# Dynamic convolution, FFT mixing and MLP on one core: the opening's DMA order, the second step's evictions, and the first three groups' transposition changed

## The chip, the cores and the metric

One NeuronCore of a Trainium2 chip runs the whole kernel. The metric is the device time of one execution in microseconds. Its engines are TensorE (PE), VectorE (DVE), ScalarE (ACT), GpSimd (POOL) and SyncE (SP), the last of which issues DMAs. Each works through its own list of instructions in order.

## The reference

x is 8 batches of 4224 positions by 192 channels; weight_gen gives 7 taps for each of 8 heads of 24 channels at every position.

```python
w = exp(weight_gen - max over taps); w = w / (sum over taps + 1e-9)
x = sum over 7 taps of w[b, s, head] * x_pad[b, s + tap, head's channels]
u = x + real(fft over channels(fft over positions(x)))
un = (u - mean(u)) / sqrt(var(u) + 1e-6)          # over the 192 channels
out = u + relu(un @ w_ch1) @ w_ch2                # 192 -> 768 -> 192
```

## The kernel before

The 4224 positions are laid out as 128 partitions by 33 rows. A batch is cut into groups of four rows (512 positions); nine groups make a batch, the last with one row, so there are 72 groups, counted through.

- `conv(b)`: the softmax of the taps (`softmax_taps`, L488 to L498), the products of taps and x (L656 on VectorE, L624 on ScalarE, L654 on GpSimd) and their sums (L666, mostly on GpSimd; in the first batch also in matmuls against the identity into pa, L662). Then row pairs are added and subtracted (sm, L680 and L682), and pg (L687) is the transform over the 128 partitions; the result is turned into gt (L694, L697) and stored to `g_d` in DRAM.
- `transform(b)`, "the second step": loads `g_d` as g2 (L722), transforms it in pp (L732) and evicts pp into the table pq, with a mirrored part and for e = 1 a sign (L736, L741, L743, L746, all on ScalarE).
- `mix(b, g)`: eo (L761) is the transform over the channels, one matmul a row and a part, added to u (ot on ScalarE at L766, then L767, L768, L770, L771 on VectorE).
- `norm(b, g)`: mean and variance (L795, L796), the root (L804), its reciprocal (L805), a shift (L808) and the normalized rows un (L813). For the MLP un is split into fp16 hi and lo parts: hl (hi at L821 on ScalarE, lo at L822 and L824), which one DMA transposes into ht (L830). For the first three groups (`QUICK`) un lies in PSUM and VectorE makes lo; later un is in SBUF and GpSimd makes it.
- `mlp(n)`: per group six chunks of 128 hidden channels. A chunk is five ph matmuls of 128x512 (L855), relu into hh (L861 for the first seven groups), then po (L878) and, at the end, u is completed (L883) and stored (L887). The first seven groups take fp32 hh and w2.

The weights are prepared in the opening: `prep_w1` rebuilds w1 from its words (L413 to L424, seven VectorE operations for a piece of 128x384), splits it into w1h and w1l (L429 ScalarE, L430 VectorE) and copies a part of it between partitions by DMA (L456). `prep_w2` does the same words for the three pieces of w2. Raw words share buffers with hl, un and ht.

The order on each engine is fixed beforehand: the generators are advanced in a written order, which sets data and buffer dependences; `held` and `behind` tie instructions to others; then `plan` places every instruction by a list scheduler with a table of costs (`cost`), and the lists it makes are what the engines run. PSUM has banks named fft (2), ph (3), po (2) and wp (1). Warm matmuls, whose results nobody reads, stand in three places (L709): 20 before the second step, 12 beside group 0's hl, 12 before group 1's MLP.

Of the kernel before, what the change touches and what calls it, by code (L numbers as in the profile page):

```python
# [46 lines left out]
F32_GROUPS = 7  # L47
ACT_TAPS = {(0, 1): (0,), (0, 3): (0,), (0, 5): (0,1), (0, 7): (0,)}
TURNS = {1: 'ddpdddd', 2: 'dpddpdd', 3: 'dpddpdp'}
WARM = (20, 0, 12, 12)  # L50
# [64 lines left out]
def cost(ins, lane, reads, writes):  # L115

    count = lambda ap: int(np.prod([n for _, n in ap.ap[1:]]))
    out = writes[0]
    n = max(map(count, reads + writes))
    if lane == "pe":  # L120
        n = count(out)
        t = 2 * max(112 if 64 < n <= DH else 56, 0.846 * n) if reads[0].dtype == F32 else max(55.5, 0.4205 * n + 0.4)
# [12 lines left out]
    return (t + 100, t + 90) if len(writes) > 1 else (t - 95, t)  # L135


def plan(nc, tc, homes, holds):
# [38 lines left out]
    spare = {row: [0.0] * homes[names[0]][2] for row, names in rows.items()}  # L177
# [110 lines left out]
def tile_dynconv_fnet_mlp(  # L288
# [158 lines left out]
    def prep_w1(raws):  # L447
        s1 = weight_scale([raw[:, :, 1] for raw in raws], 64, "w1")
        scales.append(s1)
        hi, lo = temp("w1h_1", F16), temp("w1l_1", F16)  # L450
        w = words_to_f32(raws[0], None, "w1_1", ("ph", 3))
        split_f32(w, hi, lo, s1)
        for src, dst in ((hi, w1h1), (lo, w1l1)):
            for i in range(2):
                for j in range(2):
                    nc.sync.dma_start(dst[64 * j:64 * j + 64, i * PW:(i + 1) * PW], src[64 * i:64 * i + 64])  # L456
# [61 lines left out]

    def conv(b):
# [34 lines left out]
        if b == 0:  # L554
            need_x(NC)
            need_x(0)
            tap_step(0, 7)
            need_x(1)
            need_x(3)
            load_consts()  # L560
        groups = [(NC, 0), (1, 2), (3, 4), (5, 6), (7,)] if b == 0 else [(c,) for c in range(NC + 1)]
# [142 lines left out]

    def keep_warm(bank, nm, lhsT, rhs, count):

        spare = pst(*bank, [P, 512], F32, f"warm_{nm}")
        for _ in range(count):
            nc.tensor.matmul(spare[:, 0:rhs.shape[-1]], lhsT=lhsT, rhs=rhs, start=True, stop=True)  # L709

    def transform(b):
# [5 lines left out]
        for m0 in range(0, NM, TRI):  # L717
# [4 lines left out]
            last_g2[b] = nc.sync.dma_start(g2[:, 0:full], bass.AP(first.tensor, first.offset, [[D, WL], [W * D, full], [1, D]]))  # L722
# [4 lines left out]
            for e, (tab, d0) in enumerate(((te_sb, 0), (to_sb, D - DH))):  # L727
# [8 lines left out]
                nc.scalar.copy(rows[:, k0:k0 + nk, :], pp[0:DH, 0:nk, 0:NT])  # L736
# [3 lines left out]
                if e == 0:  # L740
                    nc.scalar.copy(dst, src)  # L741
                else:
                    nc.scalar.mul(dst, src, -1.0)  # L743
# [4 lines left out]
    state, us, hls, products = {}, {}, {}, []  # L748
    last_tile, last_pg, last_product, last_fold, last_gt, last_g2, last_pp = {}, {}, {}, {}, {}, {}, {}
    pending = {}  # L750
    total = B * NG

    def mix(b, g):
# [4 lines left out]
        for e in range(2):  # L758
            for j in range(J):
                r = 2 * g + 1 + j if g < NC else 0  # L760
                nc.tensor.matmul(eo[:, e, j, :], lhsT=pq[0:DH, e, r, r:r + P], rhs=cs_sb[:, e, :],  # L761
                                 start=True, stop=True)
                yield 0.1 * (J * e + j + 1)
# [15 lines left out]
    def norm(b, g):  # L779
# [7 lines left out]
        if quick:  # L787
            halves = [pst("ph", 3, [P, 2, D], F32, f"un_{b}_{g}_{i}") for i in range(2)]
        else:
            un = sb.tile([P, 4, D], F32, tag="un", name=f"un_{b}_{g}", bufs=1)  # L790
            halves = [un[:, 0:2], un[:, 2:4]]
# [14 lines left out]
        if sign < 0:  # L806
            for t in range(T):
                nc.vector.tensor_scalar(out=rs[:, 1, t:t + 1], in0=st[:, t, 0:1], scalar1=rs[:, 0, t:t + 1], scalar2=sign,  # L808
                                        op0=ALU.mult, op1=ALU.mult)
        else:  # L810
            nc.gpsimd.tensor_tensor(out=rs[:, 1, 0:T], in0=st[:, 0:T, 0], in1=rs[:, 0, 0:T], op=ALU.mult)  # L811
        for t in range(T):
            nc.scalar.activation(halves[t // 2][:, t % 2, :], uv[:, t, :], AF.Identity,  # L813
                                 bias=rs[:, 1, t:t + 1], scale=rs[:, 0, t:t + 1])
        yield 0.5
        warm = NG * b + g == 0
        hl = sb.tile([P, 4, 2 * D], F16, tag="hl", name=f"hl_{b}_{g}", bufs=2)
        lo_eng = nc.vector if NG * b + g < QUICK else nc.gpsimd
        spans = [(un, 0, T)] if NG * b + g >= QUICK else [(h, 2 * i, 2 * i + 2) for i, h in enumerate(halves)]
        for src, t0, t1 in spans:  # L820
            nc.scalar.copy(hl[:, t0:t1, 0:D], src[:, 0:t1 - t0, :])  # L821
            lo_eng.tensor_tensor(out=hl[:, t0:t1, 2 * P:3 * P], in0=src[:, 0:t1 - t0, 0:P],  # L822
                                 in1=hl[:, t0:t1, 0:P], op=ALU.subtract)
            last_lo[NG * b + g] = lo_eng.tensor_tensor(out=hl[:, t0:t1, D:2 * P], in0=src[:, 0:t1 - t0, P:D],  # L824
                                                       in1=hl[:, t0:t1, P:D], op=ALU.subtract)
        if warm:
            keep_warm(("ph", 3), f"hl{g}", hl[:, 0, 0:P], hl[:, T - 1, 0:2 * D], WARM[2])
        hls[NG * b + g] = hl
# [102 lines left out]
    with held(last_pg[0].ins):  # L931
        WARM[0] and keep_warm(("po", 2), "pp", ident32, last_tile[0][:, 3, 0:P], WARM[0])
    add(0.0, 1.0, transform(0))
    run()
    lp = last_product[0].ins
# [5 lines left out]
    queue(lp, (prep_w1, loaded[0]))  # L941
    for i in range(2):
        queue(last_split[-1].ins, (prep_w2, i))
    for g in range(QUICK):
        add(0.0, 1.0, behind(last_split[-1].ins, mix(0, g)))
        run()
        add(0.0, 1.0, norm(0, g))
        run()
    for g, call in ((0, tap8), (1, (prep_w2, 2)), (1, tap9)):
# [14 lines left out]
    def late_warm(g):  # L964
        yield 0.0
        with held(last_ph[g - 1].ins):
            keep_warm(("ph", 3), f"hl{g}", hls[g][:, 0, 0:P], hls[g][:, 3, 0:2 * D], WARM[3])

# [11 lines left out]
    add(0.93, 0.95, late_warm(1))  # L980
# [52 lines left out]
```

## Time and profile before

| | us |
|---|---|
| median of 3 runs | 1126.27 |
| runs | 1126.01, 1126.27, 1127.51 |
| the profiled execution | 1124.56 |
| its span in the profile | 1122.8 |
| mean granted TensorE clock in it | 0.983 of full |

The page gives each engine's busy time, then the span in 40 slices, DMA queues, the chain that ended last and the costliest groups of instructions. A timeline row reads: start, length, engine, line, operation, what it writes, what it reads, shape, count, and in brackets the idle time before it with what ended that. A row of fp32 matmuls counts two passes for each matmul in its last number. Waits read: who waited for whom, the sum, how often, the longest. The profiled execution's own time is 1.76 us more than its span, and 1.71 us under the median.

### The profile page before, as it was taken

The numbers are of one execution on the slowest core, as the hardware profiler recorded it, in microseconds if no ns is written. First come the engines' busy times: TensorE is split into PE (matmuls) and PEld (weight loads), VectorE is DVE, ScalarE is ACT, GpSimd is POOL, SyncE is SP. The second block draws the span as 40 slices with busy tenths as digits, with TensorE's granted clock in tenths as the row PEclk, the third lists the DMA queues.
The fourth block names the chain that finished last, engine by engine and source line by source line (L and its number), as shares of the span: only waits on it lengthen the run. The fifth ranks groups of instructions, "written<-read, shape, count | busy, mean of one in ns | idle before, by whom it ended". The sixth has DMA issues, their size and how long they took to land.

```text
span 1122.8 us, 23426 instructions
## 1 busy us (share of the span) xinstructions
PE 1077.9 (96%) x8476; PEld 825.0 (73%) x8476; DVE 969.8 (86%) x1773; ACT 817.8 (73%) x2415; POOL 876.7 (78%) x759
## 2 busy tenths in 40 slices
PE   5986899999999999999999999999999999999998
PEld 2565487678777877787778877777778777787777
DVE  7987999779989999899999999899989999455543
ACT  4475766658986787778786888778787878689842
POOL 4979699699996999699997999599987999311200
PEclk9897799999999999999999999999999999999999
DMA  8334244533384246614474246623454222513321
GB/s 318 120 106 146 43 110 126 148 102 106 86 221 120 65 106 164 176 59 103 117 204 117 78 121 178 162 58 101 119 158 114 71 61 71 145 43 75 72 47 47
DMA packets 156500, 128.71 MB, mean 115 GB/s; under 512 B 108571, under 2 KB 133088, under 8 KB 156384
## 3 DMA queue, kind: packets, MB, share of 16 engines
q1 hardware_dynamic: 156384, 127.21, 41.6%
q8 instruction: 67, 1.10, 0.4%
q14 instruction: 49, 0.40, 0.1%
HBM read 61.46 MB, written 39.37 MB: 90 GB/s over the span
## 4 chain that ended last, share of the span: by engine, by line
PE 77%; DVE 10%; POOL 5%; issue 3%; ACT 3%; DMA 1%; SPq 0%; DVEq 0%; ACTq 0%; POOLq 0%
PE ph L855 33%; PE po L878 30%; PE eo L761 5%; PE pp L732 5%; POOL u L666 4%; PE pg L687 3%; DVE pr L656 3%; ACT pr L624 1%; PE pa L662 1%; DMA g<-g_d 1%; DVE u L666 1%; DVE u L656 1%; ACT w L491 1%; POOL sm L680 0%; DVE u L883 0%
## 5 line engine op out<-in xcount | busy, mean ns | idle before, releaser
L666 POOL TENSOR_TENSOR u<-u,pr 128x768 f32<-128x768 f32 (+1 forms) x396 | 655.5, 1673 | 53.5 <-DVE pr L656 46.2
L878 PE MATMUL po<-w2h,hh 128*128 128x192 f16 x2832 | 421.6, 246 | 0.0
L878 PEld LDWEIGHTS <-hh 128*128 128x128 f16 x4248 | 364.5, 98 | 68.2
L855 PE MATMUL ph<-ht,w1h 128*128 128x512 f16 (+1 forms) x1296 | 400.0, 363 | 3.0 <-ACT hh L861 1.5
L656 DVE TENSOR_TENSOR pr<-x_sb,wp 128x768 f32<-128x768 f32 (+1 forms) x415 | 354.0, 876 | 20.8 <-POOL u L666 16.4
L878 PE MATMUL po<-w2l,hh 128*128 128x192 f16 x1416 | 348.1, 246 | 0.0
L866 DVE SCALAR_TENSOR_TENSOR hh<-ph,hh 128x512 f16<-128x512 f32 (+1 forms) x390 | 245.1, 634 | 78.5 <-ACT hh L865 77.3
L855 PE MATMUL ph<-ht,w1l 128*128 128x512 f16 (+1 forms) x864 | 311.4, 363 | 0.0
L865 ACT ACTIVATE hh<-ph 128x512 f16<-128x512 f32 (+1 forms) x390 | 214.6, 553 | 118.7 <-PE ph L855 84.1
L855 PEld LDWEIGHTS <-w1h 128*128 128x128 f16 x1296 | 126.6, 99 | 85.8 <-DVE hl L824 2.3
L813 ACT ACTIVATE un<-u,rs 128x192 f32<-128x192 f32 x264 | 124.0, 535 | 26.6 <-POOL rs L811 21.3
L822 POOL TENSOR_TENSOR hl<-un,hl 128x512 f16<-128x512 f32 (+1 forms) x69 | 74.4, 1078 | 61.3 <-ACT hl L821 30.7
L855 PEld LDWEIGHTS <-w1l 128*128 128x128 f16 x864 | 85.7, 99 | 45.5 <-issue 3.3
L802 ACT ACTIVATE junk<-u,st 128x192 f16<-128x192 f32 x252 | 113.7, 451 | 3.8
L800 ACT ACTIVATE junk<-u 128x192 f16<-128x192 f32 x252 | 90.6, 360 | 25.3 <-DVE u L771 20.9
L761 PE MATMUL eo<-cs_sb,pq 97*128 97x97 f32 x544 | 90.8, 274 | 3.4 <-DVE u L771 3.4
L761 PEld LDWEIGHTS eo<-cs_sb,pq 97*128 97x128 f32 x544 | 83.5, 193 | 12.3 <-issue 3.6
L883 DVE SCALAR_TENSOR_TENSOR u<-po,isc,u 128x384 f32<-128x384 f32 (+1 forms) x122 | 72.7, 596 | 7.4 <-PE po L878 7.0
L680 POOL TENSOR_TENSOR sm<-u 128x382 f32<-128x382 f32 x64 | 64.3, 1005 | 7.5 <-ACT u L675 7.5
L811 POOL TENSOR_TENSOR rs<-st,rs 128x4 f32<-128x4 f32 (+1 forms) x69 | 15.4, 223 | 65.6 <-DVE rs L805 65.6
L736 ACT COPY pq<-pp 97x204 f32<-97x204 f32 (+1 forms) x96 | 46.5, 484 | 25.4 <-PE pp L732 24.2
L878 PE MATMUL po<-w2f,hh 128*128 128x192 f32 x336 | 63.8, 327 | 0.0
(108 smaller groups left out, 1295.5 us busy)
## 6 DMA issues: line engine op xcount, KB each, us to landing
out_dram<-u SPq DMA_DIRECT2D x64, 384.0 KB
x_sb<-in_x_dram SPq DMA_DIRECT2D x48, 384.0 KB
g<-g_d SPq DMA_DIRECT2D x40, 336.0 KB
x_sb<-in_x_dram SPq DMA_DIRECT2D x8, 864.0 KB
g_d<-gt SPq DMA_DIRECT2D x32, 195.0 KB
g_d<-gt SPq DMA_DIRECT2D x32, 189.0 KB
w<-in_weight_gen_dram SPq DMA_DIRECT2D x6, 924.0 KB
x_sb<-in_x_dram SPq DMA_DIRECT2D x8, 672.0 KB
```

What stands on the lines that cost most here:

```text
L656: last_product[b] = nc.vector.tensor_tensor(out=dst, in0=rows, in1=wk, op=ALU.mult)
L666: adder.tensor_tensor(out=u, in0=u, in1=pr, op=ALU.add)
L761: nc.tensor.matmul(eo[:, e, j, :], lhsT=pq[0:DH, e, r, r:r + P], rhs=cs_sb[:, e, :], start=True, stop=True)
L800: nc.scalar.activation(junk, uv[:, t, :], AF.Identity, scale=-1.0 / D, accum_out=st[:, t, 0:1])
L802: nc.scalar.activation(junk, uv[:, t, :], AF.Square, bias=st[:, t, 0:1], accum_out=st[:, t, 1:2])
L813: nc.scalar.activation(halves[t // 2][:, t % 2, :], uv[:, t, :], AF.Identity, bias=rs[:, 1, t:t + 1], scale=rs[:, 0, t:t + 1])
L822: lo_eng.tensor_tensor(out=hl[:, t0:t1, 2 * P:3 * P], in0=src[:, 0:t1 - t0, 0:P], in1=hl[:, t0:t1, 0:P], op=ALU.subtract)
L855: last_ph[n] = nc.tensor.matmul(ph[:, 0:T], lhsT=wt[:, cs_], rhs=ht[:, 0:T, blk], start=(i == 0), stop=(i == len(terms) - 1))
L865: nc.scalar.activation(a[:, 0:T], ph[:, 0:T], AF.Relu)
L866: nc.vector.scalar_tensor_tensor(out=l[:, 0:T], in0=ph[:, 0:T], scalar=0.0, in1=a[:, 0:T], op0=ALU.max, op1=ALU.subtract)
L878: nc.tensor.matmul(po[t // 2][:, t % 2, :], lhsT=hx[:, t], rhs=wx[:, c2, :], start=(c2 == 0 and i == 0), stop=(c2 == NH - 1 and i == len(t ...
L883: nc.vector.scalar_tensor_tensor(out=lt, in0=po[t // 2][:, 0:t % 2 + 1], scalar=scales[0][:, 1:2] if f32 else isc, in1=lt, op0=ALU.mult, o ...
```

## The change

The arithmetic of the result stays. What moves:

1. The planner lets the first two weight_gen loads go before the first x load on SP (`spare` starts at -1e3), and its TensorE costs change slightly.
2. Warm matmuls: 14 (identity by identity) at the very start, 40 instead of 20 before the second step, and these wait for the last pg alone, not for gt; 8 each after the mixes of groups 1 and 2; the 24 by hl go.
3. The eight w1h and w1l copies on SP stand behind the g2 load of m0 = 8.
4. In the first batch, for e = 1, the mirrored and the third copy of pp into pq go from ScalarE to VectorE (8 operations).
5. A root of one column, whose result is not used, makes ScalarE load the root's table right after the last of its pq copies.
6. The order of the first mixes and norms is written by hand: mix 1, mix 2 and their warm matmuls are issued among norm 0; w2's first two pieces use ph banks and hang on the first split of w1 instead of the last; the large softmax steps of the second batch follow groups 1 and 2 instead of 0 and 1.
7. Norm of groups 0 to 2: un lies in SBUF, two of its rows are made by ScalarE and two by VectorE; eight fp32 matmuls against the identity transpose it into two po banks; ScalarE casts these to ht's hi part and VectorE subtracts to give lo. There is no hl and no DMA transposition for these groups.

```diff
-    spare = {row: [0.0] * homes[names[0]][2] for row, names in rows.items()}
+    spare = {row: [-1e3] * homes[names[0]][2] for row, names in rows.items()}
...
-        for src, dst in ((hi, w1h1), (lo, w1l1)):
+        with held(g2_loads[0, 2 * TRI].ins):
+            for src, dst in ((hi, w1h1), (lo, w1l1)):
...
-        words_to_f32(loaded[1][i], w2_part(i)[0], f"w2_{i}", ("po", 2))
+        words_to_f32(loaded[1][i], w2_part(i)[0], f"w2_{i}", ("ph", 3) if i < 2 else ("po", 2))
...
+            if b == 0 and WARM.get(grp[0]):
+                with held(last_pg[0].ins):
+                    keep_warm(pst("po", 2, [P, P], F32, f"warm_{grp[0]}"), WARM[grp[0]])
...
+                on_dve = b == 0 and e == 1
+                last_pq[b] = nc.scalar.copy(rows[:, k0:k0 + nk, :], pp[0:DH, 0:nk, 0:NT])
...
+                elif on_dve:
+                    nc.vector.tensor_scalar_mul(out=dst, in0=src, scalar1=-1.0)
...
-                    nc.scalar.copy(rows[:, P + k0:P + k0 + n, :], pp[0:DH, 0:n, 0:NT])
+                    (nc.vector.tensor_copy if on_dve else nc.scalar.copy)(rows[:, P + k0:P + k0 + n, :], pp[0:DH, 0:n, 0:NT])
...
+        if quick:
             for t in range(T):
+                if t < ACT_ROWS:
+                    nc.vector.tensor_scalar(out=rs[:, 1, t:t + 1], ...)
+                    nc.scalar.activation(un[:, t, :], uv[:, t, :], AF.Identity, bias=rs[:, 1, t:t + 1], scale=rs[:, 0, t:t + 1])
+            for t in range(ACT_ROWS, T):
+                nc.vector.tensor_scalar(out=un[:, t, :], in0=uv[:, t, :], scalar1=st[:, t, 0:1], scalar2=rs[:, 0, t:t + 1],
+                                        op0=ALU.subtract, op1=ALU.mult)
+            yield 0.5
+            ht = sb.tile([P, 4, 3, P], F16, tag="ht", name=f"ht_{b}_{g}", bufs=3)
+            tr = [pst("po", 2, [P, 4, P], F32, f"tr_{b}_{g}_{i}") for i in range(2)]
+            R = D - P
+            for i, m in ((0, P), (1, R)):
+                for t in range(T):
+                    nc.tensor.matmul(tr[i][0:m, t, :], lhsT=un[:, t, i * P:i * P + m], rhs=ident32, start=True, stop=True)
+                nc.scalar.copy(ht[0:m, 0:T, i], tr[i][0:m, 0:T])
+                at = P - m
+                last_lo[NG * b + g] = nc.vector.tensor_tensor(out=ht[at:P, 0:T, 2 - i], in0=tr[i][0:m, 0:T],
+                                                              in1=ht[0:m, 0:T, i], op=ALU.subtract)
...
+    with held(last_pq[0].ins):
+        nc.scalar.activation(sb.tile([P, D], F16, tag="junk", name="root", bufs=2)[:, 0:1], eps_t, AF.Sqrt)
...
+    step(mixes[0])
+    step(norms[0], 1)
+    warm = pst("po", 2, [P, P], F32, "warm_eo")
+    for g in range(1, QUICK):
+        step(mixes[g], 4)
+        with held(last_mix[0].ins):
+            keep_warm(warm, WARM_EO[g - 1])
+    step(norms[0])
     for i in range(2):
-        queue(last_split[-1].ins, (prep_w2, i))
...
+        queue(last_split[0].ins, (prep_w2, i))
+    for g in range(1, QUICK):
+        step(mixes[g])
+        step(norms[g])
+        if g == 1:
+            queue(last_split[0].ins, (prep_w2, 2))
+    for g, call in zip(TAPS_AT, (tap8, tap9)):
         queue(last_lo[g].ins, call)
```

Three places show what the planner made of it. First SP, before the second step of the first batch: before, three copies of w1h stand ahead of the first g2 loads (names: `g2_0_m` is the load for m0 = m).

```order
L701 DMA g_d0_95<-gt_0_6_596 63x768
L456 DMA w1h1_89<-w1h_1_880 64x384 x3
L722 DMA g2_0_0_702<-g_d0_95 112x4x192
L722 DMA g2_0_4_720<-g_d0_95 112x4x192
L722 DMA g2_0_8_738<-g_d0_95 112x4x192
L456 DMA w1h1_89<-w1h_1_880 64x384
L456 DMA w1l1_90<-w1l_1_881 64x384 x4
L722 DMA g2_0_12_754<-g_d0_95 112x4x192
```

After, on the same engine:

```order
L712 DMA g_d0_95<-gt_0_6_611 63x768
L730 DMA g2_0_0_737<-g_d0_95 112x4x192
L730 DMA g2_0_4_755<-g_d0_95 112x4x192
L730 DMA g2_0_8_773<-g_d0_95 112x4x192
L460 DMA w1h1_89<-w1h_1_917 64x384 x4
L460 DMA w1l1_90<-w1l_1_918 64x384 x4
L730 DMA g2_0_12_789<-g_d0_95 112x4x192
```

The first three g2 loads follow the last store at once, and all eight copies stand behind them. Second TensorE, from the first mixes to the MLP, before (each of the 12 warm matmuls has its own weight load).

```order
L761 MATMUL eo_0_0_946<-cs_sb_70,pq_71 128x97 x4
L761 MATMUL eo_0_1_1003<-cs_sb_70,pq_71 128x97 x4
L761 MATMUL eo_0_2_1047<-cs_sb_70,pq_71 128x97 x4
L709 LDWEIGHTS hl_0_0_981
L709 MATMUL warm_hl0_988<-hl_0_0_981 128x384
```

After, on TensorE:

```order
L773 MATMUL eo_0_0_963<-cs_sb_70,pq_71 128x97 x4
L773 MATMUL eo_0_1_996<-cs_sb_70,pq_71 128x97 x4
L526 MATMUL warm_eo_995<-ident32_72 128x128 x8
L773 MATMUL eo_0_2_1009<-cs_sb_70,pq_71 128x97 x4
L526 MATMUL warm_eo_995<-ident32_72 128x128 x8
L829 MATMUL tr_0_0_0_1023<-ident32_72,un_0_0_977 128x128
L829 MATMUL tr_0_0_1_1024<-ident32_72,un_0_0_977 64x128
L829 MATMUL tr_0_0_0_1023<-ident32_72,un_0_0_977 128x128 x3
L829 MATMUL tr_0_0_1_1024<-ident32_72,un_0_0_977 64x128 x3
```

The first ph follows the transposes at once; group 1's transposes stand behind 13 ph matmuls of group 0, and group 2's behind the second chunk of group 1. pg_1_4 moves from 4.20 to 4.40 groups of MLP work, pp of batch 2 from 14.83 to 15.17, and pp of batch 7 stays at 60.33. Third VectorE in the second step, after; before, no row of pp stands on this engine.

```order
L752 TENSOR_SCALAR pq_71<-pp_0_0_1_747 97x11x17
L757 COPY pq_71<-pp_0_0_1_747 97x12x17
L433 SCALAR_TENSOR_TENSOR w1l0_88<-pw_w1_01_952,sc_w1_914,w1h0_87 128x384
L419 TENSOR_SCALAR pa_w2_0_1037<-raw_w3_428 128x384
L420 SCALAR_TENSOR_TENSOR pw_w2_0_1038<-pa_w2_0_1037,t_w2_0_1039 128x384
L416 TENSOR_SCALAR pa_w2_1_1047<-raw_w4_431 128x384
L752 TENSOR_SCALAR pq_71<-pp_0_4_1_765 97x12x17
L757 COPY pq_71<-pp_0_4_1_765 97x4x17
```

The eight copies stand between the words of w2's first two pieces, which came after pp before. On ScalarE, group 2's un (L819) stands between hh_0_0_0 and hh_0_0_1, and ot_0_3 ahead of hh_0_0_0.

More of the change, by code (lines that the diff above doesn't have):

```diff
@@ L517, in mirrored, with keep_warm @@
         return bass.AP(ap.tensor, ap.offset, [ap.ap[0], [step, 2], *ap.ap[1:]])
+    def keep_warm(spare, count):
+        for _ in range(count):
+            nc.tensor.matmul(spare, lhsT=ident32, rhs=ident32, start=True, stop=True)
     def conv(b):
@@ L760, in mix @@
                 r = 2 * g + 1 + j if g < NC else 0
[L761 removed]
+                last_mix[b] = nc.tensor.matmul(eo[:, e, j, :], lhsT=pq[0:DH, e, r, r:r + P], rhs=cs_sb[:, e, :],
                                  start=True, stop=True)
@@ L786, in norm @@
         quick = NG * b + g < QUICK
[L787 to L791, printed above, removed]
+        un = sb.tile([P, 4, D], F32, tag="un", name=f"un_{b}_{g}", bufs=1)
         if quick or (b > 0 and g in BN_GROUPS):
@@ L819, in norm @@
[L819 to L825, printed above, removed]
@@ L941, in tile_dynconv_fnet_mlp, with step @@
     queue(lp, (prep_w1, loaded[0]))
-    for i in range(2):
-        queue(last_split[-1].ins, (prep_w2, i))
[L944 to L949, printed above, removed]
+    mixes, norms = ([f(0, g) for g in range(QUICK)] for f in (mix, norm))
+    def step(gen, n=99):
+        for _, at in zip(range(n), gen):
+            pass
+    step(mixes[0])
[6 more added lines that the diff above has]
+    step(norms[0])
+    for i in range(2):
+        queue(last_split[0].ins, (prep_w2, i))
[5 more added lines that the diff above has]
+    for g, call in zip(TAPS_AT, (tap8, tap9)):
         queue(last_lo[g].ins, call)
```

55 lines of the change are left out of this document (25 added, 30 removed).

## The prediction

> **What bounds the kernel now.** I read the page first: how much of the span TensorE fills.
>
> ```profile
> span 1122.8 us, 23426 instructions
> PE 1077.9 (96%) x8476; PEld 825.0 (73%) x8476; DVE 969.8 (86%) x1773; ACT 817.8 (73%) x2415; POOL 876.7 (78%) x759
> ```
>
> Then the busy time by stretch, to see where the missing 45 us lie (columns: stretch, its length, each engine's busy time, granted clock, DMA share, GB/s).
>
> ```profile
> 80.00:100.00 20.00, 16.68 (x122) 15.89 (x121) 13.21 (x26) 10.00 (x26) 20.00 (x14) 0.78 0.60 165
> 100.00:120.00 20.00, 8.76 (x43) 5.71 (x42) 19.08 (x67) 11.74 (x27) 20.00 (x13) 0.65 0.27 79
> 120.00:140.00 20.00, 18.46 (x89) 11.00 (x90) 19.84 (x37) 13.22 (x35) 10.48 (x10) 0.84 0.26 40
> 400.00:1123.00 723.00, 719.83 (x6163) 556.62 (x6160) 610.42 (x1106) 552.16 (x1598) 536.14 (x475) 1.00 0.40 106
> ```
>
> From 400 us on TensorE idles 3 us in 723; between 80 and 140 us it idles 16, at a reduced clock. So after the opening the time is TensorE's work, and the kernel ends as much earlier as the MLP begins earlier, less whatever TensorE then has to wait for. Next come TensorE's waits from 75 to 360 us, and its timeline there.
>
> ```profile
> PE warm_hl L709 <- DVE st L796: 6.6, 1, 6.6
> PE pp L732 <- DMA g<-g_d: 4.7, 4, 2.7
> ```
>
> ```profile
> 79.19 6.12 PE L709 MATMUL warm_pp<-gt,ident 128*128 128x128 f32 x40 [1.23 <-DVE gt L697]
> 88.02 0.91 PE L732 MATMUL pp<-te_sb,g 102*97 102x102 f32 x8 [2.71 <-DMA g<-g_d]
> 91.71 1.57 PE L732 MATMUL pp<-to_sb,g 102*97 102x102 f32 x8
> 101.12 2.25 PE L761 MATMUL eo<-cs_sb,pq 97*128 97x97 f32 x16
> 106.05 2.00 PE L761 MATMUL eo<-cs_sb,pq 97*128 97x97 f32 x8 [2.67 <-DVE u L771]
> 119.97 0.61 PE L855 MATMUL ph<-ht,w1h 128*128 128x512 f16 x1 [1.31 <-DVE hl L824]
> 123.82 0.58 PE L855 MATMUL ph<-ht,w1h 128*128 128x512 f16 x1 [1.54 <-ACT hh L861]
> 127.30 0.36 PE L761 MATMUL eo<-cs_sb,pq 97*128 97x97 f32 x2
> 131.33 2.11 PE L709 MATMUL warm_hl<-hl 128*128 128x384 f16 x12
> 133.28 0.38 PE L855 MATMUL ph<-ht,w1h 128*128 128x512 f16 x1
> 160.07 0.38 PE L855 MATMUL ph<-ht,w1h 128*128 128x512 f16 x1
> 161.15 1.46 PE L878 MATMUL po<-w2f,hh 128*128 128x192 f32 x8
> ```
>
> The mixes of groups 0 and 1 start at 101.12, but the first MLP matmul only at 119.97: 18.9 us with a few microseconds of work in them. Group 1's first MLP matmul follows at 133.28. Between the two lie 13.3 us. At full clock five ph matmuls take 1.08 (160.07 to 161.15), so group 0's 30 take 6.5, and four eo about 0.8 (2 in 0.36 to 0.4): 7.3 us. The other 6.0 are the stall of 1.54, the 2.11 of warm_hl1, and the half clock. That the clock is halved shows in pp: 0.91 for a block, then 1.57.
>
> Last, what the first MLP matmul waits for, on the other engines' timelines.
>
> ```profile
> 82.56 1.78 SPq L456 DMA_DIRECT2D w1h<-w1h  x3
> 84.57 1.47 SPq L722 DMA_DIRECT2D g<-g_d  x3
> 95.95 0.62 DVE L430 SCALAR_TENSOR_TENSOR w1l<-pw_w,sc_w,w1h 128x384 f16<-128x384 f32 x1 [5.69 <-ACT w1h L429]
> 96.49 0.55 DVE L413 TENSOR_SCALAR pa_w<-raw_w 128x384 int32<-128x384 int32 x1
> 100.59 0.55 DVE L413 TENSOR_SCALAR pa_w<-raw_w 128x384 int32<-128x384 int32 x1
> 101.45 0.30 ACT L743 ACTIVATE pq<-pp 97x68 f32<-97x68 f32 x1
> 105.36 0.54 DVE L771 TENSOR_TENSOR u<-u,eo 128x380 f32<-128x380 f32 x1
> 107.60 0.17 DVE L796 BATCH_NORM_AGGREGATE st<-bn 128x2 f32<-128x6 f32 x1
> 108.47 1.28 ACT L804 ACT_TABLE_LOAD   x1
> 110.78 1.83 ACT L813 ACTIVATE un<-u,rs 128x192 f32<-128x192 f32 x4 [0.72 <-DVE rs L808]
> 112.54 0.84 ACT L821 CAST hl<-un 128x384 f16<-128x384 f32 x2
> 113.38 0.41 DVE L822 TENSOR_TENSOR hl<-un,hl 128x256 f16<-128x256 f32 x1
> 114.58 14.31 SPq L830 DMA_TRANSPOSE ht<-hl  x3
> ```
>
> Group 0's u is complete at 105.90, un starts at 110.78 (a table load of 1.28 sits in between), the split ends with DVE about 114.5, and the DMA transpose takes from its issue at 114.58 to 119.9: 5.3 us.
>
> **The change, part by part.** Times are those of the profiled execution.
>
> *Start.* The weight DMAs go ahead of the first x DMA. The chain of waits opens with the first row below; the last part to land decides when pa can start.
>
> ```profile
> 1.20 3.94 DMA w<-in_weight_gen_dram
> 10.19 7.25 PE pa L662 x16
> ```
>
> At best the softmax starts 2 us earlier; at worst x lands later by the same bytes and nothing comes of it. I take 1 us (0 to 2), because the products that follow also need an x piece still in flight then. The 14 warm matmuls there stand before any other TensorE work and cost nothing.
>
> *Second step.* SP no longer waits for w1h before the g2 loads, so they can issue at about 82.6 instead of 84.57, and land near 86. The 40 warm matmuls need no gt, but they stand in front of the pp: 40 at 0.235 (the 20 above took 6.12, half of that time at half clock) are 9.4, or up to 18 at half clock. From about 77 they end between 86.5 and 91; I take 87. pp then runs at full clock, but the eight moved evictions stand on VectorE between word operations. Of these the seven of w2_0 took 96.49 to 100.59, 0.585 each; 13 of them and 8 evictions at 0.3 to 0.55 are 10 to 12 us from 89, so pq is complete between 99 and 101.7, against 101.75 now. I take 101.2: nothing gained there. But the 5.69 us in which VectorE waited now hold w2's preparation, so it has none left when the mixes come, and u of group 0 is complete at about 104.9 rather than 105.9.
>
> *Norm.* The root table is loaded right after the last pq eviction, behind TensorE's eo, where ScalarE has nothing else: free by 103, and ot then starts at most 0.5 later. From u: statistics 1.9 (105.90 to 107.77 now) and 0.4 for an add of group 1 among them, root, reciprocal and two shifts 1.1 (before: 109.76 to 110.78), so un starts at 108.2 instead of 110.78. Two rows on each engine take 0.9 instead of 1.83. Eight fp32 transposes are 8 x 0.235 = 1.9, partly beside un; by eo, at 0.2 for 97 columns, 2.1; at half clock 3.8. The cast of 128x512 is near the cast row's 0.42 for 128x384, so 0.55. First ph: 108.2 + 0.5 + 1.2 + 0.6 = **110.5** instead of 119.97, 9.4 earlier.
>
> [...]
>
> *First MLP groups.* From the first ph to ph_0_1_0 TensorE now has the 7.3 us of work, transposes of group 1 (1.9), and stalls that ScalarE's order makes: hh_0_0_0 stands behind ot_0_3, which needs eo_0_3, and hh_0_0_1 behind un of group 2, which waits for VectorE. With three ph banks that is about 1.7 (0 to 5). Group 2's transposes add 1.9. So 7.3 + 1.9 + 1.7 + 1.9 = 12.8 against 13.3. **TensorE's lead is 9.4 + 0.5 = about 10 us.**
>
> *VectorE and GpSimd behind it.* VectorE gains 8 evictions (2.6), 6 rows of un (1.8, at 0.3 each) and 6 lo of 512 columns (3.8, at 0.63 each, between once and twice the 0.41 for 256 columns), and loses the old lo (6 pairs at 0.55, two of which take 113.38 to 114.5: 3.3) and six one-column shifts (about 0.8): net +4, against 5.69 of idle time now filled. The next rows show the chain that it feeds: the second batch's convolution.
>
> ```profile
> 128.08 0.94 DVE L656 TENSOR_TENSOR u<-x_sb,wp 128x768 f32<-128x768 f32 x1
> 196.96 0.22 POOL L682 TENSOR_TENSOR sm<-u 128x2 f32<-128x2 f32 x1
> 209.25 0.81 PE L687 MATMUL pg<-sm,f_sb 128*128 128x192 f32 x4
> 221.89 14.74 POOL L666 TENSOR_TENSOR u<-u,pr 128x768 f32<-128x768 f32 x8 [9.34 <-DVE pr L656]
> 850.00:950.00 100.00, 100.00 (x864) 78.47 (x863) 98.53 (x176) 80.48 (x248) 99.32 (x77) 1.00 0.27 73
> ```
>
> By the new order the first product (128.08 now) comes at about 130 to 131.5, with the mix of group 3 ahead of it that stood behind it before: 0 to 2 us later on equal terms. A sum that is ready at 197.2 is used only at 209.25, so TensorE can come up to 12 us earlier before it waits. Later the slack is thin: VectorE and GpSimd are 98 to 99% busy in the last convolution's stretch. I let TensorE give back 2 of its 10 us (0 to 8) on the way.
>
> **Sum.** 10 - 2 = 8: 1124.56 - 8 = 1116.6 for the profiled execution. That execution lay 1.7 under the median of 1126.27, so the median becomes **1118.3**.
>
> [...]
>
> **The rivals.**
>
> *All of the lead is kept* (15%). VectorE and GpSimd catch up in their idle shares (VectorE 86% over the span). 1126.3 - 10 = 1116.3, and with 2 at the start and no stalls 1113.8.
>
> *Convolution or ScalarE's order eats 4 to 7 us* (12%): pg or hh waits in the first three batches. 1126.3 - 4.5 = about 1122. For it: 98% in the quoted stretch; against: the 12 us between 197.2 and 209.25.
>
> *Half clock through the first MLP matmuls* (5%). Transposes and eo cost 1.9 more, some 3 us of ph double: 3.8 lost, 1122. It needs the 16 warm matmuls between the eo to leave a pause like the 2.67 above.
>
> *The change does little* (9%). The warm block ends at 91, the evictions wait behind word operations past 104, and the norm starts as late as now; the first ph is at 116 to 118 and stalls take the rest: 1124 to 1128.5.
>
> *Slower* (7%). The convolutions, not TensorE, set the end of each transform. VectorE starts the second convolution 3.5 late (131.6 for 128.08); busy to 98% it never catches up, and the order leaves batch 7's pp after the same share of MLP work as before, so TensorE waits there, the lead is gone and the delay shows: 1126.3 + 2.7 = 1129. It decides where the chain starts over 1 us late on equal terms and the slack of 12 us in the second batch is gone too. Against it: GpSimd's 9.34 idle before 221.89.
>
> **Chances and range.** 52% for the forecast, 1116.5 to 1120 by its own bounds. A measurement tells about 0.2% (2.25 us) from no change. Faster by more: 52 + 15 + 12 + 5 = 84%; within: 9%; slower: 7%. The range goes from the full lead, 1113.8, to 1124.5 and leaves out the slower case and most of the one where little happens, with a tail below.
>
> **What would show it.** Right: the first ph near 110.5 at full clock, no DMA transpose before it; TensorE's waits in 75 to 360 down from some 20 us to about 8; pq complete near 101; the second convolution's first product at 130 to 131.5; pp of batch 1 some 8 us earlier than 232. Wrong: idle TensorE before pg or pp of the second or third batch, ph at 0.42 each after 111, first ph after 114, or pq after 103.

## The result, and the profile after

The changed kernel takes **1138.58 us** (median of 4 runs, 1136.77 to 1139.33) against 1126.86 (4 runs, 1126.01 to 1127.51) for the kernel before: a ratio of 1.0102, 95% interval 1.0089 to 1.0115. It is 1% slower. The forecast was 1118.3. The profiled execution took 1139.18.

The head of the page, after: the span is 14.6 us longer, TensorE's and VectorE's busy times have grown by 18.7 and 16.2, and TensorE's share is the same 96%.

```profile
span 1137.4 us, 23642 instructions
PE 1096.6 (96%) x8600; PEld 837.9 (74%) x8600; DVE 986.0 (87%) x1775; ACT 813.5 (72%) x2402; POOL 876.6 (77%) x759
```

The busy time by stretch, after (same columns as above): from 100 to 120 us VectorE counts as busy for 16.90 us, but with 26 instructions where it had 67. GpSimd has no idle time there at all.

```profile
100.00:120.00 20.00, 10.37 (x81) 8.93 (x80) 16.90 (x26) 5.73 (x14) 20.00 (x13) 0.84 0.19 67
120.00:140.00 20.00, 16.33 (x78) 9.50 (x79) 18.02 (x45) 9.38 (x19) 3.42 (x5) 0.82 0.00 1
```

TensorE's waits from 75 to 360 us, after. The 6.6 us ahead of the warm matmuls on hl are gone, and the wait for g has fallen from 4.7 to 0.8; the first row is new.

```profile
PE tr L829 <- DVE un L821: 10.8, 2, 10.5
PE pg L698 <- POOL sm L693: 5.5, 5, 2.1
PE pp L740 <- DVE pq L757: 2.0, 2, 1.6
PE pp L740 <- ACT pq L757: 1.6, 2, 1.1
```

TensorE's timeline, after. pp starts at 86.98 where 87 was forecast. The transposes of group 0 begin at 110.56, stop for 10.46 us, and the first MLP matmul comes at 125.62: forecast 110.5, before 119.97. pp does not keep the full clock that was forecast: after a wait of 1.63 us for an eviction on VectorE, five blocks take 1.34 to 1.66 us, where one at full clock takes 0.86 to 0.94; the granted clock was 0.64 from 92 to 96 us and 0.50 from 96 to 100.

```profile
78.05 9.09 PE L526 MATMUL warm<-ident 128*128 128x128 f32 x80
86.98 0.86 PE L740 MATMUL pp<-te_sb,g 102*97 102x102 f32 x8
...
92.17 0.91 PE L740 MATMUL pp<-to_sb,g 102*97 102x102 f32 x8 [1.63 <-DVE pq L757]
...
94.65 1.65 PE L740 MATMUL pp<-to_sb,g 102*97 102x102 f32 x8 [0.39 <-DVE pq L757]
...
110.56 1.27 PE L829 MATMUL tr<-ident,un 128*128 128x128 f32 x6 [0.54 <-ACT un L819]
122.29 0.79 PE L829 MATMUL tr<-ident,un 128*128 128x128 f32 x2 [10.46 <-DVE un L821]
...
125.62 0.61 PE L874 MATMUL ph<-ht,w1h 128*128 128x512 f16 x1
...
129.24 2.41 PE L829 MATMUL tr<-ident,un 128*128 128x128 f32 x16
```

VectorE's timeline, after. The two rows of un that were priced at 0.3 each take 13.40 us together for group 0; group 1's two, beside an idle GpSimd (0.00 busy from 124 to 150 us), take 0.66. The statistics of the same u (first row), also from SBUF to SBUF, took 0.33 beside the same busy GpSimd. Further down is the second convolution's first product.

```profile
107.75 0.33 DVE L803 BATCH_NORM_STATS2 bn<-u 128x6 f32<-128x192 f32 x1
...
109.96 13.40 DVE L821 TENSOR_SCALAR un<-u,st,rs 128x192 f32<-128x192 f32 x2
...
127.83 0.66 DVE L821 TENSOR_SCALAR un<-u,st,rs 128x192 f32<-128x192 f32 x2
...
148.04 0.95 DVE L667 TENSOR_TENSOR u<-x_sb,wp 128x768 f32<-128x768 f32 x1
```

All six instructions of that line, after, as the view of one line gives them (shortest, median, longest in ns): one instruction of 12.278 us among others of 0.37.

```profile
L821 DVE TENSOR_SCALAR un<-u,st,rs x6: 371/375/12278, 110.0 to 135.0; 128x192 f32<-128x192 f32 x6
```

GpSimd's timeline, after, at the end of that instruction. The 12.278 us begin at 109.96 and end at 122.24, 0.12 after the end of GpSimd's L677 (122.12) and while its small L693 runs; from 100 us on GpSimd has had no idle time. The second row of un ends at 123.36, 0.11 after L691.

```profile
119.36 1.01 POOL L691 TENSOR_TENSOR sm<-u 128x382 f32<-128x382 f32 x1
120.31 1.81 POOL L677 TENSOR_TENSOR u<-u,pr 128x768 f32<-128x768 f32 x1
122.06 0.23 POOL L693 TENSOR_TENSOR sm<-u 128x2 f32<-128x2 f32 x1
122.26 0.99 POOL L691 TENSOR_TENSOR sm<-u 128x382 f32<-128x382 f32 x1
```

The 11.9 us that this instruction took beyond the shortest show neither as idle time nor in the table of VectorE's waits: VectorE counts as busy. They show in the spread between median and longest (0.375 and 12.278), and in the count of instructions in a stretch (26 for 67).

### The profile page after: what moved, and what is told of

Read it like the earlier page. It is cut to its first block, busy times and chain, and to the rows that moved or that the text cites. A ratio compares the mean times of both kernels' runs of the same rounds, so it can differ in the third digit from the quotient of the medians.

```text
span 1137.4 us, 23642 instructions
## 1 busy us (share of the span) xinstructions
PE 1096.6 (96%) x8600; PEld 837.9 (74%) x8600; DVE 986.0 (87%) x1775; ACT 813.5 (72%) x2402; POOL 876.6 (77%) x759
## 4 chain that ended last, share of the span: by engine, by line
PE 71%; POOL 10%; DVE 9%; issue 4%; ACT 3%; DMA 3%; SPq 0%; POOLq 0%; ACTq 0%; DVEq 0%
PE ph L874 31%; PE po L897 28%; POOL u L677 8%; PE pp L740 4%; PE eo L773 4%; PE pg L698 3%; DVE pr L667 2%; ACT pr L635 1%; DVE un L821 1%; POOL sm L691 1%; DMA g<-g_d 1%; DMA x_sb<-in_x_dram 1%; DMA f_sb<-in_f_dram 1%; DVE wp L497 1%; DVE hh L885 0%
## 5 line engine op out<-in xcount | busy, mean ns | idle before, releaser
L677 POOL TENSOR_TENSOR u<-u,pr 128x768 f32<-128x768 f32 (+1 forms) x396 | 657.3, 1678 | 47.8 <-DVE pr L667 39.7
L839 ACT ACTIVATE un<-u,rs 128x192 f32<-128x192 f32 x252 | 118.8, 538 | 21.1 <-POOL rs L837 18.5
L773 PEld LDWEIGHTS eo<-cs_sb,pq 97*128 97x128 f32 x544 | 78.9, 191 | 6.9 <-issue 0.6
L773 PE MATMUL eo<-cs_sb,pq 97*128 97x97 f32 x544 | 83.4, 271 | 0.3 <-DVE pq L752 0.2
L691 POOL TENSOR_TENSOR sm<-u 128x382 f32<-128x382 f32 x64 | 65.6, 1025 | 8.1 <-ACT u L686 7.9
L698 PE MATMUL pg<-sm,f_sb 128*128 128x192 f32 x256 | 55.8, 341 | 8.1 <-POOL sm L693 8.1
```

The source lines that it names most:

```text
L677: adder.tensor_tensor(out=u, in0=u, in1=pr, op=ALU.add)
L691: nc.gpsimd.tensor_tensor(out=sm[:, :, 1:D], in0=u[:, 0:2, 1:D], in1=u[:, 3:1:-1, D - 1:0:-1], op=ALU.add)
L698: last_pg[b] = nc.tensor.matmul(pg[:, j, :], lhsT=f1_sb[:, t2 + j, :], rhs=sm[:, j, :], start=True, stop=True)
L773: last_mix[b] = nc.tensor.matmul(eo[:, e, j, :], lhsT=pq[0:DH, e, r, r:r + P], rhs=cs_sb[:, e, :], start=True, stop=True)
L839: nc.scalar.activation(un[:, t, :], uv[:, t, :], AF.Identity, bias=rs[:, 1, t:t + 1], scale=rs[:, 0, t:t + 1])
```

## The experiments

Two questions were open: what holds the two rows of un, and why, even without that, the forecast lead does not arrive. The runs are put together here. "First ph" is the start of the first MLP matmul, "chain start" that of the second convolution's first product on VectorE; both, and the span, are in us of the profiled execution, which lies up to 2.3 us from that run's median. The ratio is to runs of the kernel before made beside each.

| run | median us (runs) | ratio to before, 95% | first ph | chain start | span | span minus chain start |
|---|---|---|---|---|---|---|
| before | 1126.86 (4) | 1 | 119.97 | 128.1 | 1122.8 | 994.7 |
| after | 1138.58 (4) | 1.0102 (1.0089, 1.0115) | 125.6 | 148.0 | 1137.4 | 989.4 |
| act4 | 1125.48 (11) | 0.9984 (0.9975, 0.9993) | 114.2 | 134.4 | 1124.2 | 989.8 |
| act3 | 1136.25 (2) | 1.0082 (1.0064, 1.0101) | 122.4 | 144.8 | 1133.6 | 988.8 |
| imm | 1142.11 (2) | 1.0134 (1.0115, 1.0154) | 129.9 | 151.6 | 1142.4 | 990.8 |
| stt | 1139.66 (4) | 1.0111 (1.0097, 1.0125) | 127.7 | 150.0 | 1138.8 | 988.8 |
| stt_ps | 1126.38 (12) | 0.9999 (0.9985, 1.0012) | 114.5 | 136.2 | 1125.4 | 989.2 |
| pool_off | 1132.94 (2) | 1.0057 (1.0037, 1.0076) | 115.9 | 139.5 | 1130.6 | 991.1 |
| act4_ev | 1122.47 (6) | 0.9960 (0.9945, 0.9975) | 112.0 | 132.3 | 1121.3 | 989.0 |
| ev_open | 1123.13 (6) | 0.9967 (0.9953, 0.9980) | 113.3 | 133.6 | 1122.5 | 988.9 |
| act4_taps | 1126.46 (12) | 0.9995 (0.9987, 1.0003) | 114.2 | 132.7 | 1124.7 | 992.0 |
| ev_now2 | 1122.38 (5) | 0.9962 (0.9948, 0.9975) | 112.5 | 130.7 | 1121.4 | 990.7 |
| b_late | 1127.87 (12) | 1.0007 (0.9994, 1.0020) | 119.6 | 127.8 | 1124.0 | 996.2 |
| b_late2 | 1135.46 (6) | 1.0076 (1.0058, 1.0094) | 121.9 | 139.5 | 1133.7 | 994.2 |

### What holds the rows of un

**act4** gives all four rows of un to ScalarE, **act3** three of them (`ACT_ROWS = 3`).

```diff
-ACT_ROWS = 2
+ACT_ROWS = 4
```

> Edit: all four un rows of the first three groups on ScalarE, none on VectorE (ACT_ROWS = 4). Theory 1 (VectorE's un row at L821 cannot run while GpSimd runs without a gap, and waits until that run ends at 122): the 12 us go, first ph at 113 to 114.5, first product of the second convolution at about 135 instead of 148, time 1119 to 1124. Theory 2 (VectorE's added work, not this wait, makes the convolution late): only the 2 us of the rows themselves go, time 1133 or more.

> Edit: one un row of four on VectorE instead of two (ACT_ROWS = 3). Theory 1 (wait until GpSimd's run ends): the one row takes 11 to 12.5 us in group 0, first ph at 123 to 125, time 1135 to 1139. Rival (each such row is slow by itself, some 6 us on average): half of the stall, first ph near 119, time near 1131.

act4 is 13.1 us faster than after and its first ph comes 11.4 earlier: the stall is worth the whole loss against before. The time is still 1.5 us above the range that was expected. With act3 the single row left to VectorE still takes 12.31 us (first fence, VectorE), and ends at 119.97, 0.13 after GpSimd's L677 (second fence, GpSimd; 118.04 and 1.80 make 119.84) and again while L693 runs. Half the work, the same wait: it is not work that became slow, but a wait up to a moment that GpSimd sets.

```profile
107.66 12.31 DVE L821 TENSOR_SCALAR un<-u,st,rs 128x192 f32<-128x192 f32 x1
```

```profile
118.04 1.80 POOL L677 TENSOR_TENSOR u<-u,pr 128x768 f32<-128x768 f32 x1
119.80 0.22 POOL L693 TENSOR_TENSOR sm<-u 128x2 f32<-128x2 f32 x1
```

**imm** keeps the instruction but takes its two per-partition scalars away. It leaves out the normalization of rows 2 and 3 in groups 0 to 2. **stt** keeps the arithmetic in another form of instruction, with a second tensor from SBUF.

```diff
-nc.vector.tensor_scalar(out=un[:, t, :], in0=uv[:, t, :], scalar1=st[:, t, 0:1], scalar2=rs[:, 0, t:t + 1],
+nc.vector.tensor_scalar(out=un[:, t, :], in0=uv[:, t, :], scalar1=0.0, scalar2=1.0,
```

```diff
-nc.vector.tensor_scalar(out=un[:, t, :], in0=uv[:, t, :], scalar1=st[:, t, 0:1], scalar2=rs[:, 0, t:t + 1],
-                        op0=ALU.subtract, op1=ALU.mult)
+nc.vector.scalar_tensor_tensor(out=un[:, t, :], in0=uv[:, t, :], scalar=st[:, t, 0:1],
+                               in1=rs[:, 0, t:t + 1].broadcast_to([P, D]), op0=ALU.subtract, op1=ALU.mult)
```

> Edit: the two VectorE rows of un by the same tensor_scalar with two constants (0 and 1) instead of the two scalars per partition; this leaves out the normalization of rows 2 and 3 in groups 0 to 2. Theory 1 (the single-tensor operation from SBUF to SBUF waits for GpSimd): the first takes 11 us or more and ends near 122, time 1136 to 1140. Rival (the scalars per partition make it slow): 0.37 each, first ph at 112 to 114, time 1118 to 1123.

> Edit: the two VectorE rows of un by scalar_tensor_tensor, u less the mean (a scalar per partition) times the root's reciprocal read as a second SBUF tensor (stride 0), instead of tensor_scalar. Theory 1 in the form that only the single-tensor operation waits for GpSimd (TENSOR_TENSOR of 128x768 at L656 takes 0.94 with GpSimd busy): rows of 0.35 to 0.6, first ph at 112 to 114, time 1118 to 1123. Theory 1 in the wider form, that two SBUF inputs wait as well: the stall stays, 1136 to 1140. Rival (scalars per partition are what is slow): the stall stays or is half.

Both still wait. The line's view for each, imm and then stt: 0.22 and 0.41 us when free, 13.87 and 12.40 in group 0. Neither the scalar operands nor one form of instruction is the cause: all three forms of un whose tensors lie in SBUF alone waited. Both come out within 4 us of after, and do nothing for the time.

```profile
L821 DVE TENSOR_SCALAR un<-u x6: 221/240/13867, 109.6 to 137.5; 128x192 f32<-128x192 f32 x6
```

```profile
L821 DVE SCALAR_TENSOR_TENSOR un<-u,st,rs x6: 408/412/12395, 111.8 to 137.0; 128x192 f32<-128x192 f32 x6
```

**stt_ps** is stt with one operand, the reciprocal, in PSUM (spare columns of the wp bank): it asks whether the wait needs every tensor in SBUF.

```diff
+rp = wbanks[1][:, 488 + 4 * g:492 + 4 * g]
+nc.vector.reciprocal(out=rp[:, 2:4], in_=rs[:, 0, 2:4])
...
-                               in1=rs[:, 0, t:t + 1].broadcast_to([P, D]), op0=ALU.subtract, op1=ALU.mult)
+                               in1=rp[:, t:t + 1].broadcast_to([P, D]), op0=ALU.subtract, op1=ALU.mult)
```

> Edit: the two VectorE rows of un by scalar_tensor_tensor as in stt, but the root's reciprocal is written to PSUM and read from there, so that only one tensor is read from SBUF. [...] Rival (it is the un tile or its place that makes the wait): first row 10 us or more, time 1136 to 1141.

The wait is gone: the rows take 0.39 and 0.41 us (first fence, VectorE), beside a GpSimd that is as busy as in after (second fence, GpSimd). The time falls by 13.3 us against stt. One operand in PSUM is the only difference in those instructions; it is enough.

```profile
110.89 0.39 DVE L824 SCALAR_TENSOR_TENSOR un<-u,st,wp 128x192 f32<-128x192 f32 x1
111.19 0.33 DVE L820 TENSOR_SCALAR rs<-st,rs 128x1 f32<-128x1 f32 x2
111.44 0.41 DVE L824 SCALAR_TENSOR_TENSOR un<-u,st,wp 128x192 f32<-128x192 f32 x1
```

```profile
109.03 1.82 POOL L677 TENSOR_TENSOR u<-u,pr 128x768 f32<-128x768 f32 x1
110.82 1.53 POOL L665 TENSOR_TENSOR pr<-x_sb,w 128x768 f32<-128x768 f32 x1
```

**pool_off** leaves un as in after and thins out GpSimd: the second batch's c = 1 goes from GpSimd to VectorE.

```diff
-POOL_TAPS = {(0, 0): (5, 6), (0, 1): (5, 6), (0, 3): (6,), (1, 0): range(7), (1, 1): range(7)}
+POOL_TAPS = {(0, 0): (5, 6), (0, 1): (5, 6), (0, 3): (6,), (1, 0): range(7)}
```

> Edit: the changed kernel, with the second batch's second piece (c = 1) taken from GpSimd, so that its run of work without a gap ends near 100 instead of 123. Theory 1: the first un row on VectorE (L821) takes 0.4 to 1.5 instead of 12.3. Rival (the wait has nothing to do with GpSimd): still 10 us or more. The time itself is no test, since the products of c = 1 go to VectorE: 1125 to 1140.

The longest row of un falls to 1.72 us (the line's view, pool_off), so the wait goes with GpSimd's work. It is a little more than the 0.4 to 1.5 expected, and ends 0.12 after a GpSimd sum (113.48) that was running when the row began. The time does not fall back to act4's, as VectorE now has the moved sums and the chain starts at 139.5.

```profile
L821 DVE TENSOR_SCALAR un<-u,st,rs x6: 370/378/1724, 111.9 to 126.0; 128x192 f32<-128x192 f32 x6
```

### Why act4 gains 1.4 us and not 8

In act4 the first ph is 5.8 us earlier than before, and the time is 1.4 shorter. **act4_ev** gives the eight evictions back to ScalarE; **ev_open** also takes back the opening's DMA order and its 14 warm matmuls.

```diff
-                on_dve = b == 0 and e == 1
+                on_dve = False
```

```diff
-WARM = {-1: 14, 7: 40}
+WARM = {7: 40}
...
-    spare = {row: [-1e3] * homes[names[0]][2] for row, names in rows.items()}
+    spare = {row: [0.0] * homes[names[0]][2] for row, names in rows.items()}
```

> Edit: as act4, and the eight evictions of the second step are on ScalarE again. Theory A: VectorE is done sooner by 1 to 3 us, first product at 131 to 133.5, span 1120 to 1123, time 1122 to 1124.5. Rival: ScalarE's evictions hold pp longer, pq complete after 104, time 1126 or more.

> Edit: as act4_ev, with the opening's DMA order and its 14 warm matmuls taken back. The first pa started at 10.19 before and at 9.96 to 11.04 in six runs with the new order, so the order is worth nothing: first pa at 10 to 10.5, time within 1 us of act4_ev (1121.5 to 1123.5). Rival (my forecast's term): 1 us or more slower than act4_ev.

Undoing the evictions gains 3.0 us, and 1122.47 is under both kernels. VectorE's timeline, after, shows why they cost: the eviction at 91.21 reads a pp bank that was full when the matmul at 87.68 ended, about 88.5; it stands behind word operations, and TensorE waits for the bank (the two pp rows among the waits above). The clock was lower with these waits as well. In after TensorE was busy for 1.49 of the 4 us from 88 to 92, and its granted clock was 0.64 and 0.50 in the next two stretches of 4 us. From 80 to 100 us the clock was 0.83 in act4, where pp waited 1.6 us at the longest, and 1.00 in act4_ev, where it waited 1.0. So a block of pp takes 0.90 to 0.94 there (second fence, TensorE, act4_ev) against up to 1.66 in act4. pq is complete at 103.54 in after, 103.67 in act4 and 100.83 in act4_ev.

```profile
90.75 0.55 DVE L418 SCALAR_TENSOR_TENSOR t_w<-raw_w,pa_w 128x384 int32<-128x384 int32 x1
91.21 0.47 DVE L752 TENSOR_SCALAR pq<-pp 97x187 f32<-97x187 f32 x1
```

```profile
96.06 0.90 PE L740 MATMUL pp<-to_sb,g 102*97 102x102 f32 x8
```

The opening's order is worth 0.7 us between two medians whose intervals overlap: nothing that could be told apart.

**act4_taps** moves the large softmax steps of the second batch one group earlier. **b_late** and **b_late2** take the kernel before, with its other order, and repeat one reciprocal of the softmax six times, to delay VectorE's convolution without touching TensorE's opening. **ev_now2** is act4_ev with less VectorE work ahead of that convolution: five of the seven operations that rebuild the third piece of w2 are left out, and a third of w2 holds other numbers.

```diff
-TAPS_AT = (1, 2)
+TAPS_AT = (0, 1)
```

```diff
-            nc.vector.reciprocal(out=m[:, sl], in_=m[:, sl])
+            for _ in range(7 if b == 1 and n > 100 else 1):
+                nc.vector.reciprocal(out=m[:, sl], in_=m[:, sl])
```

```diff
     def prep_w2(i):
+        if i == 2:
...
+            nc.vector.tensor_scalar(out=a, in0=raw[:, :, 1], scalar1=0x3FF00000, scalar2=None, op0=ALU.bitwise_and)
+            last_word.append(nc.vector.tensor_tensor(out=w2_part(i)[0].bitcast(I32), in0=a, in1=raw[:, :, 0], op=ALU.bitwise_and))
+            return
```

> Edit: as act4 (all un rows on ScalarE), and the second batch's large softmax steps follow groups 0 and 1 again, as before the change (TAPS_AT = (0, 1)). Theory A (in every run so far the profiled span was the start of the second convolution's first VectorE product plus 988.6 to 989.8, but 994.7 before the change: the convolutions on VectorE and GpSimd set the end, and before the change TensorE did by 6 us): first product at 128 to 131 instead of 134.4, span 1117 to 1120, time 1119 to 1122. Theory B (TensorE's own start sets the end): no change against act4, 1125.5.

> Edit on the kernel before: six more reciprocals of 128x192 (1.35 each) of the second batch's softmax sum, an even number, on VectorE just ahead of the second convolution's first product; nothing else waits for them. First product near 136.2 instead of 128.1. Theory A: 136.2 + 989.3 = span 1125.5, 2 to 3 us over before (time 1128.5 to 1130). Theory B (TensorE-bound, the convolution has slack): no change, 1126.9. A convolution without slack already before: 8 us over, 1135.

> Edit on the kernel before, as b_late was meant: six more reciprocals of 128x192 (1.35 each, an even number) on VectorE right ahead of the second convolution's first product; the MLP's start does not hang on them. First product near 136 instead of 128.1, first ph unchanged near 120. Theory A (the convolutions on VectorE and GpSimd set the end: in act4, act4_ev and stt_ps the last pg stands 828.7 to 829.7 after that product, before the change 834.9, so that it had 6 us to spare): last pg at 965 to 966, 2 to 3 us later than before, time 1128.5 to 1130. Theory B (TensorE sets it, slack is larger): no change, 1126.9. No slack: 1135.

> Edit: as act4_ev, and five of the seven VectorE operations that rebuild the third piece of w2 ahead of the second convolution's first product are left out, so that the last third of w2 holds other numbers. The first ph does not wait for them. Theory A: first product 2.3 us earlier, at 129.5 to 130.5, time 2 to 2.5 under act4_ev, 1120 to 1120.7. Theory B: first ph at 112 as in act4_ev, time unchanged, 1122.5.

b_late missed its aim: with the condition `hi == N2` the repeats fell on a small 128x32 piece near 80 us, the chain start stayed at 127.8, and the run says nothing about a delay. b_late2 (`n > 100`) hit the 128x192 piece: VectorE's chain starts 11.4 us later than before (139.52, first fence, b_late2). Of these, 1.9 are there at the first ph already. About 2 more come from the planner, which placed everything behind the reciprocals anew: the mix of group 3 now stands ahead of the chain (132.20), where before it began at 129.94, behind the first product. The median grew by 8.7 us against the kernel before beside it (1126.73), which fits the 1135 expected for no slack. So there was no slack of 6 or 12 us to use up, and the start of TensorE's work alone did not set the time: a delay on VectorE is passed on for the most part. As the order behind it changed too, the run is not a delay of the convolution alone. At the start of the third convolution the delay is 13.1 (233.08 there, against 219.99 in the second fence, before).

```profile
132.20 0.30 DVE L768 TENSOR_TENSOR eo<-eo,ot 128x194 f32<-128x194 f32 x1
...
139.52 0.95 DVE L657 TENSOR_TENSOR u<-x_sb,wp 128x768 f32<-128x768 f32 x1
...
233.08 0.95 DVE L657 TENSOR_TENSOR u<-x_sb,wp 128x768 f32<-128x768 f32 x1
```

```profile
219.99 0.95 DVE L656 TENSOR_TENSOR u<-x_sb,wp 128x768 f32<-128x768 f32 x1
```

In the changed order, with a chain start anywhere from 130.7 to 151.6, the span is the chain start and 989 to 992. That alone does not show that the chain decides, for the span less the first ph is nearly as even: 1009 to 1012.5 in all these runs but pool_off (1014.7). Only pool_off parts the two: it differs from act4 by 1.7 in the first ph, by 5.1 in the chain start and by 6.4 in the span. In act4 VectorE reaches the chain at 134.39, behind group 2's lo and the softmax's reciprocal:

```profile
128.53 0.69 DVE L832 TENSOR_TENSOR ht<-tr,ht 128x512 f16<-128x512 f32 x1 [1.05 <-ACT ht L830]
...
132.57 1.35 DVE L502 RECIPROCAL wp<-wp 128x192 f32<-128x192 f32 x1
133.96 0.40 DVE L598 TENSOR_TENSOR wp<-w,wp 128x224 f32<-128x224 f32 x1
134.39 0.95 DVE L667 TENSOR_TENSOR u<-x_sb,wp 128x768 f32<-128x768 f32 x1
```

Against before that is 6.3 later. The new order needs 4.9 us less behind the chain start (994.7 less 989.8), so act4's span is 1.4 longer than before's (1124.2 for 1122.8). The medians differ by 1.4 the other way, because before's profiled execution lay 2.3 under its median and act4's 0.5 over its own: the 4.9, taken from one execution each, is uncertain by some 3 us.

The other direction does not hold. act4_taps and ev_now2 start the chain 1.7 and 1.6 earlier than act4 and act4_ev, with the first ph within 0.5, and no time is gained (1126.46 for 1125.48, 1122.38 for 1122.47): theory A, by which the chain sets the end, failed in both. The third convolution starts within 0.3 of the other's (224.9 for 225.15, 223.3 for 223.1); what holds it there when the second starts earlier was not found.

The traces narrow down where TensorE's lead goes. The first pp of batch 1 starts at 232.57 before, 228.13 in act4 and 226.29 in act4_ev; the first pp of batch 7 at 971.48, 972.57 and 969.65. A lead of 4.4 us has become a lag of 1.1, and one of 6.3 has shrunk to 1.8, though TensorE counts as busy for over 99% of the time from 300 to 1000 us in all three. The loss stands inside that busy time. Which waits make it was not shown.

## Why the prediction was wrong

**The step that failed: "Two rows on each engine take 0.9 instead of 1.83."** ScalarE's two did (0.98, at 109.96), VectorE's took 13.40. The price of 0.3 is near the 0.37 of such a row when nothing holds it; what the sum left out is the wait for GpSimd. The change put un, u and the scalars all in SBUF, beside a GpSimd that ran without a gap, and the prediction shows no row of this instruction in that place. The statistics that stood there (0.33 us at 110.30, before) read SBUF without a wait, so they gave no warning. A cost that no row shows wanted bounds from both sides; it got one value. The stall was in none of the rivals either. Its size is 13.1 us (after against act4) or 13.3 (stt against stt_ps), more than the whole 11.7 by which the change is slower.

**Without the stall the forecast would still have been 7.2 us too low** (act4's 1125.48 for 1118.3). Two terms make this up.

- *"pq is complete between 99 and 101.7 ... I take 101.2: nothing gained there."* It was complete at 103.54. The sum counted VectorE's operations and not the bank that TensorE needs back; two evictions queued behind word operations held the next pp (1.63 and 0.39 us, after). "pp then runs at full clock" failed too: five blocks ran at a granted clock of 0.64 and 0.50 (after, 92 to 100 us). Worth 3.0 us together (act4 against act4_ev).
- *"So after the opening the time is TensorE's work, and the kernel ends as much earlier as the MLP begins earlier"*, with 2 of 10 us given back. In act4 and act4_ev the MLP begins 5.8 and 8.0 us earlier than before, and the time is only 1.4 and 4.4 shorter; in b_late2 a delay on VectorE was passed on for the most part. The 12 us that one sum lay ready before its pg, in the second batch, were slack in one place and not in the whole. The forecast of the chain start, 130 to 131.5, was in the text, but priced at 0 to 2. If the 989 to 992 of the table hold, it gives a span of 1119 to 1123.5 and, with the 1.8 outside the span, an estimate of 1121 to 1125: a gain of 1 to 6 where 8 was forecast. The 4.2 us by which act4_ev still misses the forecast fit this term. That they are all of it is argued, not shown, and how the lead is lost stays open.

The rival "slower" had the direction right by luck. Its convolution starts late and never catches up, which gave 1129; but the slowness came from the stall, which it lacked, and without the stall the change was no slower than before (act4 1125.48, stt_ps 1126.38).

**What was right.** The start of pp (86.98 for 87) and the warm block (9.09 for 9.4). The opening's order, taken as 1 us out of 0 to 2, was nothing: pa starts at 9.96, before at 10.19. From u complete (106.95) to un 3.0 us passed, forecast 3.3. The root's load costs ot 0.5 us, as forecast: ot_0_0 starts 1.93 after the first eo, before 1.40. Eight transposes took 2.41, forecast 1.9; a lo of 512 columns 0.69, forecast 0.63. With the stall away the first ph came at 114.2 to 114.5 and, with the evictions back, at 112.0; 110.5 was forecast, so the path on TensorE did become some 6 to 8 us shorter. That the clock would be full at the transposes and the first ph was the author's estimate; without the stall it was (act4: 1.00 from 100 to 120 us, first ph 0.38). TensorE's waits from 75 to 360 us sum to 11.5 in act4 (forecast about 8), 24.7 in after. What the forecast named as signs against it came: first ph after 114 and at 0.61 us instead of act4's 0.38, pq after 103, and idle TensorE before pg (5.5 us in five waits). pp of batch 1, forecast some 8 us earlier than 232, came at 241.83 in after and 4.4 us earlier than before in act4.

## What to carry to other kernels

When an operation moves to VectorE, note for each operand whether it lies in SBUF or PSUM, and look at what GpSimd does at that moment: here three forms with SBUF tensors alone waited (11.9 to 13.6 us), one with an operand in PSUM did not (0.39), and neither did the statistics (0.33), so the price has to come from the very instruction in the very place. An engine that is busy all the time later on (TensorE here, over 99% from 300 to 1000 us) doesn't prove that an earlier start of its work is passed to the end: read its lead at several points (here 4.4 us at batch 1 and none at batch 7). A start time whose distance to the end stays the same in every run is a suspect and no proof, as two start times had that here; move each alone, both ways, and see that the order behind it has stayed. A stall can hide in busy time, so read the longest instruction of a group beside its median (here 12.28 us beside 0.37).

## What the runs showed of the hardware

- A VectorE instruction that made un (128x192) from tensors that all lay in SBUF waited 11.9 to 13.6 us for GpSimd (after, act3, stt, imm; the longest less the free one), in after over eight GpSimd instructions of at most 1.81 us each; stt's instruction with one operand in PSUM took 0.39 beside the same work (stt_ps). How GpSimd's work holds up the one and not the other was not shown.
- The statistics of the same u (L803, SBUF to SBUF) did not wait: 0.33 us at 107.75 in after, beside the same GpSimd work.
- In after, act3, imm and stt the first row of un ends 0.12 to 0.21 us after the large GpSimd instruction ahead of the first L693, one of two elements a partition, and at none of the borders between large ones before it.
- Elsewhere a VectorE instruction on SBUF tensors was held up for less. In after, VectorE's sum of two SBUF tensors took 1.56 at 170.00 (first fence, VectorE; 0.95 at 151.50, where GpSimd is idle) and ended at 171.56, while GpSimd ran three sums in 6.10 up to 175.02 (second fence, GpSimd). Why the sum took 0.6 us longer there, and un's row 11.9 us longer between 110 and 122 us, stays open.
- The granted TensorE clock was 0.64 and 0.50 in after from 92 to 96 and from 96 to 100 us, after 4 us in which TensorE was busy for 1.49 and waited 1.63 at the longest. From 80 to 100 us it was 0.83 in act4, where TensorE was busy for 17.30 of the 20 us, and 1.00 in act4_ev, busy for 17.77.

The two rows of the sum at 170.00, after:

```profile
170.00 1.56 DVE L677 TENSOR_TENSOR u<-u,pr 128x768 f32<-128x768 f32 x1
```

```profile
168.92 6.10 POOL L677 TENSOR_TENSOR u<-u,pr 128x768 f32<-128x768 f32 x3
```
